# Splitting the left-over tokens one block ahead of their matmuls, into tiles of their own

## The chip, the core and the metric

The kernel runs on one core of one Trainium2 chip. The metric is device time in microseconds (us) for one whole execution. A core has a matrix engine (TensorE; PE in the profile, and PEld for its weight loads), a vector engine (VectorE, DVE), an activation engine (ScalarE, ACT), and a queue that issues DMA transfers (SP). Each engine works through its own instructions in order and waits for the others through semaphores.

## The reference, cut to what matters

A two-step attention makes one row of 512 numbers for each of 8 x 576 = 4608 tokens, and a feed-forward block with the Mish activation follows:

```python
p_packed = sm_attn(p, k, v)            # 32 packed rows per batch and head
out = sm_attn(q, p_packed, p_packed)   # batch 8, heads 8, seq 576, head_dim 64
x = out.transpose(0, 2, 1, 3).reshape(4608, 512)
h = x @ w_in                           # 512 -> 2048
g = h * np.tanh(softplus(h))           # Mish
return g @ w_out                       # 2048 -> 512
```

## The kernel before, in words

**Arithmetic.** A float32 operand of the large products is split into a high part (cast to a shorter float) and a low part (operand minus high part). Three matmuls, high x high, high x low, low x high, stand for one (`down_one`, L403 to L407). Every split therefore needs a copy that casts and a subtraction.

**Tiling.** The main loop (L501) runs over 8 batches x 16 pieces of 128 hidden features, called groups, and two further turns that drain it. One turn of the loop is called a block here, and f is the group's number within its batch. In block t the kernel

- computes the hidden values of group t in two halves of 288 tokens (`up`, L379): six matmuls each into a `ps_h` bank of PSUM, of which there are two, then Mish on ACT (L391);
- splits 512 of the 576 tokens into `g_hi` and `g_lo` on DVE (`halves`, L397, with L400 and L401);
- multiplies group t-2 (`dn` in the code; LAG is 2) with `w_out`, four chunks of 128 tokens, three matmuls each, into four PSUM accumulators held over all 16 groups of a batch (`down`, L419);
- moves the attention of the next batch a few steps on (`next(gen)`); these steps use the two-bank PSUM pool `ps_a`, ACT and DVE. In the blocks with f % 4 == 2, `packed_w` (L331) makes the next piece of the folded input weights, in the same pool.

**The left-over tokens.** 576 is not a multiple of 128: 64 tokens remain per batch. Mish for them goes to a tile `g_rest` (L393), four groups side by side. Two batches, an even and an odd one, are put together so that 64 + 64 fill 128 rows. When `dn` is the last of four groups of an odd batch (L542), `down_rest` (L437) splits both `g_rest` tiles (`split`, L357: two casts on ACT, L362, and two subtractions on DVE, L363), runs twelve matmuls into a `ps_a` bank, and copies the bank to, or adds it on, the tile `o_rest` (L446, L449). That happens 16 times: four odd batches with four sets of four groups. The block in which it happens has f = 5, 9, 13 of the same odd batch, or f = 1 of the batch after it. In the last batch, there being no next one, the fourth happens in the second draining turn.

**Buffers.** `split_tiles` (L354) hands out `g_hi` and `g_lo` tiles with GB = 3 buffers of each. `halves` and `split` take from the same three. At the time of a `down_rest`, groups t, t-1 and t-2 hold one each; group t-2 gives its own back with its last matmul, the one just ahead of `down_rest`.

**What sets the order.** Only PE's order is written out by hand (`manual_schedule`, L474): it follows the text of the loop. The order of ACT and DVE, and which of them makes an `nc.any` copy, is chosen when the kernel is built, by a planner that prefers what stands earlier in the text among the instructions that it takes to be ready. On the chip each engine then keeps its order. The lines at the end of a block read:

```python
            if grp:
                grp.up(1)
                grp.halves()
            if dn:
                down(dn, 3)
            ...
            if dn and dn.b % 2 == 1 and dn.f % 4 == 3:
                down_rest(dn)
```

Of the kernel before, what the change touches and what calls it, by code (L numbers as in the profile page):

```python
# [9 lines left out]
F32R = mybir.dt.float32r  # L10
# [7 lines left out]
GB = 3  # L18
# [10 lines left out]
def body(  # L29
# [16 lines left out]
    P = 128  # L46
# [8 lines left out]
    MAIN = NCH * P  # L55
# [8 lines left out]
    moe = ctx.enter_context(tc.tile_pool(name="moe", bufs=2))  # L64
# [38 lines left out]
    def psum(pool, shape, name):  # L103
        return pool.tile(shape, F32, name=name, tag="acc" if pool is ps_acc else "ps_a")
# [221 lines left out]
    def fetch_wi(b, c):  # L326
        for g in range(2):
            wis[b, c, g] = wts.tile([P, 2, FC], F32, name="wi", tag="w32", bufs=4)
            nc.sync.dma_start(out=wis[b, c, g], in_=w_in_f32[c][:, g])

    def packed_w(b, c):  # L331

        ppTb = batches[b].ppT
        ps = [ps_a.tile([P, FC], F32, name=f"ps_w{g}", tag="ps_a") for g in range(2)]
        for h in range(4):
            for g in range(2):
                row = ((h % 2) ^ g) * D
                nc.tensor.matmul(  # L338
                    out=ps[g][h * NP:(h + 1) * NP, :],
                    lhsT=ppTb[row:row + D, g, h * NP:(h + 1) * NP],  # L340
                    rhs=wis[b, c, g][row:row + D, h // 2, :],
                    start=True, stop=True,
                    tile_position=(row, h * NP),
                )
        halves = []
        for g in range(2):
            hi = wts.tile([P, FC], F32R, name="wp_hi", bufs=4)
            lo = wts.tile([P, FC], F32R, name="wp_lo", bufs=4)
            nc.scalar.copy(out=hi, in_=ps[g])  # L349
            nc.vector.tensor_tensor(out=lo, in0=ps[g], in1=hi.bitcast(F32), op=ALU.subtract)  # L350
            halves.append((hi, lo))
        return halves

    def split_tiles():  # L354
        return [moe.tile([P, MAIN], F32R, name=n, bufs=GB) for n in ("g_hi", "g_lo")]

    def split(*srcs):  # L357

        hi, lo = split_tiles()
        for n, src in enumerate(srcs):  # L360
            h, l = (x.rearrange("p (f u t) -> p u f t", u=len(srcs), f=src.shape[1])[:, n] for x in (hi, lo))
            nc.scalar.copy(out=h, in_=src)  # L362
            nc.vector.tensor_tensor(out=l, in0=src, in1=h.bitcast(F32), op=ALU.subtract)  # L363
        return hi, lo

    class Group:
# [30 lines left out]
        def halves(self):  # L397
            self.g = split_tiles()
            hi, lo = self.g
            nc.vector.tensor_copy(out=hi, in_=self.act)  # L400
            nc.vector.tensor_tensor(out=lo, in0=self.act, in1=hi.bitcast(F32), op=ALU.subtract)  # L401

    def down_one(acc, hi, lo, cs, f, start, stop):  # L403
        wh, wl = wo_hi[f], wo_lo[f]
        nc.tensor.matmul(out=acc, lhsT=hi[:, cs], rhs=wh, start=start, stop=False)  # L405
        nc.tensor.matmul(out=acc, lhsT=hi[:, cs], rhs=wl, start=False, stop=False)  # L406
        nc.tensor.matmul(out=acc, lhsT=lo[:, cs], rhs=wh, start=False, stop=stop)  # L407
# [11 lines left out]
    def down(grp, c):  # L419
        b, f, g = grp.b, grp.f, grp.g  # L420
        if f == 0 and c == 0:
            accs[:] = [ps_acc.tile([P, DO], F32, name=f"acc{i}", tag="acc") for i in range(NCH)]
        down_one(accs[c], g[0], g[1], slice(c * P, (c + 1) * P), f, f == 0, f == NF - 1)
        if f < NF - 1:
            return
        o = evac(accs[c], c)
        a = c * P
        while a < (c + 1) * P:
            n = a // R
            e = min((n + 1) * R, (c + 1) * P)  # L430
            si = 2 * (n % NI) + n // NI
            nc.sync.dma_start(out=out_v[b, si, a - n * R:e - n * R, :], in_=o[a - c * P:e - c * P, :])
            a = e

    rest = {}

    def down_rest(grp):  # L437

        i = grp.f // 4
        hi, lo = split(grp.g_rest[0][i], grp.g_rest[1][i])  # L440
        ps = psum(ps_a, [P, DO], "ps_rest")
        for t in range(4):
            down_one(ps, hi, lo, slice(t * P, (t + 1) * P), 4 * i + t, t == 0, t == 3)
        if i == 0:
            rest["o"] = moe.tile([P, DO], F32, name="o_rest", bufs=1)
            nc.scalar.copy(out=rest["o"], in_=ps)  # L446
            return
        o = rest["o"]
        nc.vector.tensor_tensor(out=o, in0=ps, in1=o, op=ALU.add)  # L449
        if i == NF // 4 - 1:  # L450
            for u in range(2):
                nc.sync.dma_start(
                    out=out_v[grp.b - 1 + u, SI - 1, R - REST:R, :], in_=o[u * REST:(u + 1) * REST, :]
                )

    def together(*gens):
        gens = list(gens)
        while gens:
            gens = [x for x in gens if next(x, "end") != "end"]
# [9 lines left out]
    def convert(n):  # L469
        for fn, *args in weights[:n]:  # L470
            fn(*args)
        del weights[:n]

    with tc.manual_schedule(engines={mybir.EngineType.PE}):  # L474
        for _ in range(8):
            nc.tensor.matmul(out=ps_warm, lhsT=still, rhs=still, start=True, stop=True)
        first = batches[0]
        first.load()
        convert(2)
        first.start(ps_a)  # L480
        together(first.score(0, ps_acc))
        first.exps(slice(0, 1))
        together(first.score(1, ps_acc))
        first.exps(slice(1, 2))
        together(first.turn(0, ps_a))
        convert(2)
        together(first.turn_weights(0, ps_acc))
        together(first.turn(1, ps_a))
        together(first.turn_weights(1, ps_acc))
        together(first.values(0, ps_acc), first.values(1, ps_acc))  # L490
        together(first.turn_values(0, ps_a), first.turn_values(1, ps_a))
        together(first.match(0, ps_acc), first.match(1, ps_acc))
        for g in range(2):
            first.weigh(slice(g, g + 1))
        wps = {(0, 0): packed_w(0, 0)}
        convert(5)
        batches[1].load()
        groups = []
        gen = iter(())
        g_rest = None  # L500
        for t in range(n_groups + LAG):  # L501
            b, f = divmod(t, NF)
            grp = None
            if t < n_groups:
                if f == 0:
                    if b % 2 == 0:
                        g_rest = ([], [])
                if f == (0 if b else 2) and b + 1 < B:
                    gen = batches[b + 1].attention()
                if f == 10 and b + 2 < B:  # L510
                    batches[b + 2].load()
                grp = Group(b, f, wps[b, f // 4], g_rest)
                grp.tiles()
            groups.append(grp)
            dn = groups[t - LAG] if t >= LAG else None
            if b == 0:
                convert(2)
            if dn:
                down(dn, 0)
            if grp:  # L520
                grp.up(0)
            next(gen, None)
            if dn:
                down(dn, 1)
                down(dn, 2)
            next(gen, None)
            if grp:
                grp.up(1)
                grp.halves()
            if dn:  # L530
                down(dn, 3)
            if grp and f % 4 == 2:
                nb, nch = divmod(b * (NF // 4) + f // 4 + 1, NF // 4)
                if nb < B:
                    if nb > b:
                        together(gen)
                    wps[nb, nch] = packed_w(nb, nch)
                    if nb + (nch + 1) // 4 and nb + (nch + 1) // 4 < B:
                        fetch_wi(nb + (nch + 1) // 4, (nch + 1) % 4)
            else:  # L540
                next(gen, None)
            if dn and dn.b % 2 == 1 and dn.f % 4 == 3:  # L542
                down_rest(dn)
# [26 lines left out]
```

## Time and profile before

| what | value |
|---|---|
| time of 3 runs | median 862.61 us, 859.67 to 862.83 |
| the profiled execution | 864.72 us, of which its span (first to last instruction) is 862.6 us |
| mean granted TensorE clock | 0.957 of full speed |
| PE busy | 91% of the span |
| DVE, ACT busy | 49%, 39% |
| DMA queue of the data | 34.2% of 16 DMA engines' span |

Durations below come from the profiled execution. In a row of the timeline the first number is the start in us from the span's start, the second how long it took; then follow the engine, the line of the kernel, the operation, what is written <- what is read, the shape, how many instructions of that kind are merged in the row, and in brackets how long the engine stood idle before and which instruction ended that. Matmuls overlap each other in the records, so that the distance from one start to the next is shorter than the duration. In a row of the stage table come the stretch, its length, the busy time of PE, PEld, DVE, ACT and POOL, each with its number of instructions, the granted clock of PE, the share of the DMA engines, and GB/s.

### The profile page before, as it was taken

To read this page: it belongs to the slowest core of one execution; us is meant where nothing else is said; L and a number is where in the kernel's file an instruction comes from. 1 tells how busy PE (TensorE), PEld (TensorE's weight loads), DVE (VectorE), ACT (ScalarE), POOL (GpSimd) and SP (SyncE) were. 2 spreads that over 40 slices of the span, in tenths; PEclk is the share of its full clock that TensorE was granted. 3 is DMA by queue.
4 is the path that set the end of the run, shared out by engine and by line. 5 is a ranking of instruction groups with operands and counts; after the bars stand their busy time and mean duration, and the time that the engine had idled before them with its cause. 6 is when DMAs were issued, how large, how long until landed. Compare 5 with 4: busy or idle time off the path is not lost.

```text
span 862.6 us, 13789 instructions
## 1 busy us (share of the span) xinstructions
PE 782.9 (91%) x5584; PEld 614.0 (71%) x5584; DVE 421.3 (49%) x812; ACT 335.2 (39%) x766; POOL 0.7 (0%) x6
## 2 busy tenths in 40 slices
PE   6508679999989999999989999999989999999997
PEld 4306567777767787777767777877767777887776
DVE  4788984743453335544453344544363344532332
ACT  3556673435332353335232353335242352332221
POOL 0000000000000000000000000000000000000000
PEclk9857879999989999999999999999999999999999
DMA  9957753243311433153311343144300431131002
GB/s 260 273 204 226 239 184 85 65 154 93 105 50 49 123 105 105 49 154 109 105 50 49 96 132 105 49 132 131 105 28 31 125 95 51 50 98 49 1 1 61
DMA packets 43966, 90.02 MB, mean 104 GB/s; under 512 B 8576, under 2 KB 27008, under 8 KB 43904
## 3 DMA queue, kind: packets, MB, share of 16 engines
q1 hardware_dynamic: 43904, 89.15, 34.2%
q8 instruction: 44, 0.72, 0.3%
q14 instruction: 18, 0.15, 0.1%
HBM read 75.50 MB, written 13.63 MB: 103 GB/s over the span
## 4 chain that ended last, share of the span: by engine, by line
PE 79%; DVE 7%; DMA 7%; ACT 4%; issue 2%; SPq 0%; DVEq 0%; ACTq 0%
PE ps_h L388 22%; PE acc L405 14%; PE acc L407 13%; PE acc L406 13%; PE ps_w L338 3%; PE ps_kq L118 3%; DMA w_st<-in_moe_w_in_dram 3%; PE ps_rest L407 2%; PE ps_s L127 2%; DMA w_st<-in_moe_w_out_dram 2%; PE ps_rest L406 2%; PE ps_rest L405 2%; PE ps_pp L209 1%; DVE g_lo L363 1%; DVE g_hi L400 1%
## 5 line engine op out<-in xcount | busy, mean ns | idle before, releaser
L391 ACT ACTIVATE g<-ps_h 128x288 f32<-128x288 f32 (+1 forms) x256 | 98.5, 385 | 322.6 <-PE ps_h L388 260.7
L405 PE MATMUL acc<-wo_hi,g_hi 128*128 128x512 f32 x512 | 217.5, 425 | 0.0
L406 PE MATMUL acc<-wo_lo,g_hi 128*128 128x512 f32 x512 | 204.0, 398 | 0.0
L407 PE MATMUL acc<-wo_hi,g_lo 128*128 128x512 f32 x512 | 203.7, 398 | 0.0
L400 DVE CAST g_hi<-g 128x512 fp32r<-128x512 f32 x128 | 54.6, 426 | 268.2 <-ACT g L391 268.2
L388 PE MATMUL ps_h<-aT_hi,wp_hi 128*128 128x288 f32 x512 | 159.2, 311 | 23.2 <-ACT aT_hi L263 22.6
L388 PE MATMUL ps_h<-aT_lo,wp_hi 128*128 128x288 f32 x512 | 152.9, 299 | 1.9 <-DVE aT_lo L264 1.9
L388 PE MATMUL ps_h<-aT_hi,wp_lo 128*128 128x288 f32 x512 | 152.9, 299 | 0.0
L405 PEld LDWEIGHTS acc<-wo_hi,g_hi 128*128 128x128 f32 x512 | 97.7, 191 | 42.9 <-issue 23.7
L388 PEld LDWEIGHTS ps_h<-aT_hi,wp_hi 128*128 128x128 f32 x512 | 97.9, 191 | 40.6 <-ACT aT_hi L263 24.1
L407 PEld LDWEIGHTS acc<-wo_hi,g_lo 128*128 128x128 f32 x512 | 97.4, 190 | 23.8
L388 PEld LDWEIGHTS ps_h<-aT_lo,wp_hi 128*128 128x128 f32 x512 | 98.2, 192 | 11.3 <-DVE aT_lo L264 2.6
L406 PEld LDWEIGHTS acc<-wo_lo,g_hi 128*128 128x128 f32 x512 | 98.1, 192 | 8.8
L388 PEld LDWEIGHTS ps_h<-aT_hi,wp_lo 128*128 128x128 f32 x512 | 98.1, 192 | 0.0
L401 DVE TENSOR_TENSOR g_lo<-g,g_hi 128x512 fp32r<-128x512 f32 x128 | 88.3, 690 | 6.1
L350 DVE TENSOR_TENSOR wp_lo<-ps_w,wp_hi 128x512 fp32r<-128x512 f32 x64 | 41.4, 684 | 21.2 <-ACT wp_hi L349 21.2
L349 ACT CAST wp_hi<-ps_w 128x512 fp32r<-128x512 f32 x64 | 34.4, 591 | 33.8 <-PE ps_w L338 33.8
L405 PE MATMUL ps_rest<-wo_hi,g_hi 128*128 128x512 f32 x64 | 29.4, 459 | 12.7 <-ACT g_hi L362 12.6
L407 PE MATMUL ps_rest<-wo_hi,g_lo 128*128 128x512 f32 x64 | 29.8, 466 | 8.7 <-DVE g_lo L363 8.7
L338 PE MATMUL ps_w<-wi,ppT 64*32 64x512 f32 x512 | 35.7, 606 | 0.0
L118 PE MATMUL ps_kq<-ident,k_t 96*128 96x96 f32 x192 | 26.6, 270 | 9.2 <-issue 5.5
L118 PE MATMUL ps_kq<-ident,q_t 96*128 96x96 f32 x192 | 27.0, 270 | 8.4 <-issue 3.1
(81 smaller groups left out, 725.4 us busy)
## 6 DMA issues: line engine op xcount, KB each, us to landing
wi<-w_in_f SPq DMA_DIRECT2D x56, 512.0 KB, 4.5
k_t<-in_k_dram SPq DMA_DIRECT2D x32, 288.0 KB, 3.7
q_t<-in_q_dram SPq DMA_DIRECT2D x32, 288.0 KB, 5.0
v_t<-in_v_dram SPq DMA_DIRECT2D x32, 288.0 KB, 3.5
w_st<-in_moe_w_in_dram SPq DMA_DIRECT2D x16, 512.0 KB, 5.3
w_st<-in_moe_w_out_dram SPq DMA_DIRECT2D x16, 512.0 KB, 4.4
out_dram<-o SPq DMA_DIRECT2D x24, 192.0 KB, 2.6
w_in_f<-wi SPq DMA_DIRECT2D x8, 512.0 KB, 5.0
```

Of the source, the lines that this page charges most:

```text
L118: nc.tensor.transpose(out=ps[:, h, :], in_=of_slot(src, g, h)[:, i, :], identity=ident[:R, :R])
L127: nc.tensor.matmul(out=ps[u][h * NP:(h + 1) * NP, :], lhsT=packT[u * D:(u + 1) * D, h * NP:(h + 1) * NP], rhs=xT[u * D:(u + 1) * D, :, h, ...
L338: nc.tensor.matmul(out=ps[g][h * NP:(h + 1) * NP, :], lhsT=ppTb[row:row + D, g, h * NP:(h + 1) * NP], rhs=wis[b, c, g][row:row + D, h // 2 ...
L349: nc.scalar.copy(out=hi, in_=ps[g])
L350: nc.vector.tensor_tensor(out=lo, in0=ps[g], in1=hi.bitcast(F32), op=ALU.subtract)
L388: nc.tensor.matmul(out=ps, lhsT=w[:, fs], rhs=a[:, g, cs], start=(n == 0), stop=(n == 5))
L391: nc.scalar.activation(out=self.act[:, hf * HALF:hf * HALF + m], in_=ps[:, :m], func=AF.Mish)
L400: nc.vector.tensor_copy(out=hi, in_=self.act)
L401: nc.vector.tensor_tensor(out=lo, in0=self.act, in1=hi.bitcast(F32), op=ALU.subtract)
L405: nc.tensor.matmul(out=acc, lhsT=hi[:, cs], rhs=wh, start=start, stop=False)
L406: nc.tensor.matmul(out=acc, lhsT=hi[:, cs], rhs=wl, start=False, stop=False)
L407: nc.tensor.matmul(out=acc, lhsT=lo[:, cs], rhs=wh, start=False, stop=stop)
```

## The change

The tile maker gets a name and a number of buffers. `halves` keeps its three buffers of `g_hi` and `g_lo`; `split` gets one buffer each of two new tiles, `r_hi` and `r_lo`. The call of `split` moves out of `down_rest`, where `dn.f % 4 == 3`, to the block before, where `dn.f % 4 == 2`: after the `halves` of that block's group and ahead of its `down(dn, 3)`. `down_rest` picks up the finished tiles.

```diff
-    def split_tiles():
-        return [moe.tile([P, MAIN], F32R, name=n, bufs=GB) for n in ("g_hi", "g_lo")]
+    def split_tiles(name="g", bufs=GB):
+        return [moe.tile([P, MAIN], F32R, name=f"{name}_{n}", bufs=bufs) for n in ("hi", "lo")]
 
     def split(*srcs):
 
-        hi, lo = split_tiles()
+        hi, lo = split_tiles("r", 1)
...
     def down_rest(grp):
 
         i = grp.f // 4
-        hi, lo = split(grp.g_rest[0][i], grp.g_rest[1][i])
+        hi, lo = rest["g"]
...
                 grp.up(1)
                 grp.halves()
+            if dn and dn.b % 2 == 1 and dn.f % 4 == 2:
+                rest["g"] = split(dn.g_rest[0][dn.f // 4], dn.g_rest[1][dn.f // 4])
             if dn:
                 down(dn, 3)
```

## The prediction

> **What bounds the kernel now.** I read the page first, for the span; then the groups of PE's instructions for the stretch from 200 us to the last matmul; then PE's waits; then the timeline around single places.
>
> ```profile
> span 862.6 us, 13789 instructions
> ```
>
> All left-over work lies behind 200 us. In that stretch PE's groups read as follows (line, engine, names, shape, count | busy us, mean ns | idle us ahead of them and who ended it):
>
> ```profile
> L405 PE MATMUL acc<-wo_hi,g_hi 128*128 128x512 f32 x439 | 183.6, 418 | 0.0
> ...
> L388 PE MATMUL ps_h<-aT_lo,wp_hi 128*128 128x288 f32 x430 | 126.6, 294 | 0.0
> L407 PE MATMUL ps_rest<-wo_hi,g_lo 128*128 128x512 f32 x64 | 29.8, 466 | 8.7 <-DVE g_lo L363 8.7
> L405 PE MATMUL ps_rest<-wo_hi,g_hi 128*128 128x512 f32 x64 | 29.4, 459 | 12.7 <-ACT g_hi L362 12.6
> ```
>
> The reader is to see that PE, the engine that sets the end, has no idle time to speak of in its large groups, and that the two that do wait are matmuls of `ps_rest`, the left-over tokens: first for the cast of L362, then for the subtraction of L363. These two lines are what the change moves. The view of PE's waits gives their number (us in total, times, longest):
>
> ```profile
> PE ps_h L388 <- ACT aT_hi L263: 22.6, 2, 17.0
> PE ps_rest L405 <- ACT g_hi L362: 12.6, 12, 2.8
> PE ps_rest L407 <- DVE g_lo L363: 8.7, 15, 1.3
> ```
>
> The wait above them, for the first batch's attention, lies at the start of the kernel and isn't touched. 15 of the 16 places wait: three each at f = 5, f = 9 and f = 1, and six with no attention beside them, at f = 13 and in the last batch. The sixteenth, in the draining turns, doesn't. Its split on ACT and then its first matmuls on PE show what a place costs when the split is done early:
>
> ```profile
> 849.49 0.71 ACT L362 CAST g_hi<-g_rest 128x256 fp32r<-128x256 f32 x2
> ```
> ```profile
> 854.89 0.39 PE L407 MATMUL acc<-wo_hi,g_lo 128*128 128x512 f32 x1
> 855.13 0.39 PE L405 MATMUL ps_rest<-wo_hi,g_hi 128*128 128x512 f32 x1
> 855.36 0.39 PE L406 MATMUL ps_rest<-wo_lo,g_hi 128*128 128x512 f32 x1
> ```
>
> There the matmuls start every 0.23 us, from the main product into the left-overs without a break. An ordinary place, in a block with no attention beside it, looks like this, PE first, then ACT, then DVE:
>
> ```profile
> 264.11 0.40 PE L407 MATMUL acc<-wo_hi,g_lo 128*128 128x512 f32 x1
> 265.07 0.50 PE L405 MATMUL ps_rest<-wo_hi,g_hi 128*128 128x512 f32 x1 [0.56 <-ACT g_hi L362]
> 265.40 0.40 PE L406 MATMUL ps_rest<-wo_lo,g_hi 128*128 128x512 f32 x1
> 266.18 0.50 PE L407 MATMUL ps_rest<-wo_hi,g_lo 128*128 128x512 f32 x1 [0.38 <-DVE g_lo L363]
> ```
> ```profile
> 264.31 0.71 ACT L362 CAST g_hi<-g_rest 128x256 fp32r<-128x256 f32 x2
> ```
> ```profile
> 265.37 0.75 DVE L363 TENSOR_TENSOR g_lo<-g_rest,g_hi 128x256 fp32r<-128x256 f32 x2
> ```
>
> The cast begins 0.20 us after the start of the last matmul that reads group t-2's buffer: it was waiting for that buffer, since the three are taken. PE then has the cast and the subtraction in front of it. The worst places, three of them, are those in the block with f = 9:
>
> ```profile
> 236.38 0.40 PE L407 MATMUL acc<-wo_hi,g_lo 128*128 128x512 f32 x1
> 239.60 0.80 PE L405 MATMUL ps_rest<-wo_hi,g_hi 128*128 128x512 f32 x1 [2.83 <-ACT g_hi L362]
> ```
> ```profile
> 236.00 1.17 ACT L252 ACTIVATE a<-a 128x1152 f32<-128x1152 f32 x1 [0.33 <-DVE a L249]
> 237.19 1.28 ACT L391 ACT_TABLE_LOAD   x1
> ...
> 238.84 0.71 ACT L362 CAST g_hi<-g_rest 128x256 fp32r<-128x256 f32 x2
> ```
>
> Here the buffer is free at about 236.6 us, but ACT is in the exponentials of the next batch's second softmax, then loads the table for Mish, and comes to the cast 2.2 us later. In the block with f = 1 it is DVE that is late:
>
> ```profile
> 290.57 0.40 PE L406 MATMUL ps_rest<-wo_lo,g_hi 128*128 128x512 f32 x1
> 292.28 0.50 PE L407 MATMUL ps_rest<-wo_hi,g_lo 128*128 128x512 f32 x1 [1.31 <-DVE g_lo L363]
> ```
>
> **What the waits cost now.** The idle time understates it, in three ways.
>
> Idle time: 12.6 + 8.7 = 21.3 us.
>
> Overlap: an undisturbed matmul takes 0.39 us by the record and the next starts after 0.23. A wait also loses the 0.16 that would have overlapped. 12 + 15 = 27 waits x 0.16 = 4.3 us.
>
> Refilling: after a wait the second matmul follows 0.33 us after the first (265.07 to 265.40) and not 0.23. 27 waits x 0.10 = 2.7 us. As a check, the ordinary place has 0.56 + 0.38 + 2 x 0.16 + 2 x 0.10 = 1.46 us, and by starts alone, from 264.11 to 266.18, it has 2.07 - 3 x 0.23 = 1.38, to which the refill behind 266.18 (0.10) comes: 1.48.
>
> The clock: the stage table for the stretches around four of the places shows the granted clock of PE (the number ahead of the last two):
>
> ```profile
> 238.93:245.76 6.83, 6.00 (x13) 4.30 (x14) 5.68 (x11) 1.71 (x5) 0.00 (x0) 0.50 0.00 0
> 485.00:488.10 3.10, 1.74 (x9) 1.01 (x9) 2.65 (x7) 1.10 (x3) 0.00 (x0) 1.00 0.78 246
> 488.10:491.50 3.40, 3.40 (x10) 2.66 (x9) 0.00 (x0) 0.00 (x0) 0.00 (x0) 0.50 0.04 11
> 434.00:436.90 2.90, 0.73 (x2) 0.30 (x2) 2.58 (x7) 1.68 (x5) 0.00 (x0) 1.00 0.00 0
> 436.91:440.32 3.41, 3.20 (x8) 2.53 (x9) 2.64 (x4) 0.67 (x1) 0.00 (x0) 0.50 0.00 0
> 631.50:634.88 3.38, 1.52 (x5) 0.97 (x6) 3.06 (x8) 1.15 (x5) 0.00 (x0) 1.00 0.00 0
> 634.88:638.29 3.41, 3.41 (x9) 2.64 (x8) 1.36 (x3) 0.67 (x1) 0.00 (x0) 0.50 0.00 0
> 236.80:239.60 2.80, 0.00 (x0) 0.00 (x0) 2.08 (x4) 2.72 (x6) 0.00 (x0) 0.88 0.00 0
> 265.00:268.60 3.60, 3.15 (x12) 2.29 (x13) 1.12 (x3) 0.02 (x1) 0.00 (x0) 1.00 0.00 0
> ```
>
> After the three 2.83 us waits at f = 9, and after one of the three at f = 1, PE works at half clock for 3.4 or 6.8 us. After an ordinary place (last row) it doesn't. PE was busy 6.00 + 3.40 + 3.20 + 3.41 = 16.0 us at half clock; work that takes 16.0 us there takes 8.0 at full clock, so at most 8 us are lost. A part of that busy time is fixed latency, which need not halve, so I take 7.
>
> Together 21.3 + 4.3 + 2.7 + 7 = 35.3 us, all on PE. At f = 9 alone it is 3 x (2.83 + 0.16 + 0.10) = 9.3 for the first wait, about 2 for the second (of the 8.7, six ordinary places take 6 x 0.38 and three at f = 1 take 3 x 1.31, which leaves 2.5 for those at f = 5 and f = 9, and overlap and refill come to it), and 12.6 x 0.5 = 6.3 less a little for the clock: 17 us.
>
> The Trainium skill, page "TensorE: Matmul & The Clock Gate", section "HAM oscillation — how this bites in real kernels", has the clock fall only when PE stands idle for longer than about 3.4 us. This trace differs: 2.83 us idle had half clock behind it three times, and 1.31 us (487.7 us, the third row) once. By that rule the half clock isn't the doing of these waits, and the saving would be without its 7 us; it is a rival below.
>
> **The change, part by part.**
>
> Removed: the wait for group t-2's buffer. With tiles of its own the split needs only `g_rest`, finished a block earlier: the fourth of the groups, dn + 1, had its Mish in the block before the one in which the split now stands. The single `r` buffer was last read four blocks earlier, so it adds no wait. Saved at the 12 places outside f = 9: all that they cost now, 35.3 - 17 = 18.
>
> Moved: per place two casts on ACT, 0.71 us together, and two subtractions on DVE, 0.75, to the block before; no DMA goes with them. That block has f = 4, 8, 12 or 0, without exponentials. The matmuls come at the end of the next block, which first has twelve main matmuls (12 x 0.23 = 2.8 us) and two halves of the up product to do. So casts and subtractions, 1.5 us one behind the other, have twice their time or more. The stretches in which I expect them (one of each kind):
>
> ```profile
> 203.50:205.60 2.10, 2.10 (x17) 1.90 (x16) 1.07 (x2) 0.51 (x2) 0.00 (x0) 1.00 0.03 7
> 231.40:233.90 2.50, 2.50 (x27) 1.82 (x27) 2.43 (x5) 0.00 (x0) 0.00 (x0) 1.00 0.00 0
> 260.10:262.60 2.50, 2.50 (x15) 2.14 (x14) 0.86 (x2) 0.41 (x1) 0.00 (x0) 1.00 0.00 0
> 283.50:286.00 2.50, 2.50 (x19) 2.27 (x18) 1.07 (x2) 1.44 (x5) 0.00 (x0) 1.00 0.00 0
> ```
>
> ACT has 1.06 to 2.50 us free in each, enough for 0.71. DVE has over 1.0 us free in three, enough for 0.75; only behind f = 8 (second row, 2.43 of 2.50 busy) does it push something back: the transposes and the maximum of the second softmax, by up to 0.75 us. Queued behind it are the exponentials and the Mish of f = 9. The Mish is needed for a `ps_h` bank only two halves later, and DVE is rid of the same 0.75 us one block on. If that cover is gone, each of the three costs 0.75.
>
> Bounds of the moved part: nothing at the lower end (it can't gain, being the same instructions), and at the upper end 16 x (0.71 + 0.75) = 23 us if PE waited for all of it. Nearest is the last place, whose split ran at 849.49 us, 5 us ahead of its matmuls, with no wait of PE's behind it: nothing. I take 0.5 us at each of the three f = 8 places: 1.5.
>
> What is late next at f = 9: PE's twelve matmuls now begin at once and the following block comes 6 us sooner, towards `packed_w` at f = 10. That wants two `ps_a` banks, one of which is free only when the add of L449 has run on DVE, which is then in the softmax. I expect it to fit between two steps of that chain.
>
> Sum: 35.3 - 1.5 = 34 us (33.8). The profiled execution's 864.72 us would become 831; it lies 2.1 over the median of the runs, 862.61, so that the median would become 829.
>
> **The rivals.**
>
> *The waits at f = 9 stay in another form.* The add of L449, or the Mish of f = 10, sits in its engine's order behind the softmax's chain, and PE waits for a PSUM bank. For it: that chain holds ACT with the exponentials of 236.00 us, and DVE has its subtractions, sums and transposes of it (DVE is busy for 5.68 of 6.83 us in the first row of the stage table). Against: the planner chooses the order anew. Saving 34 - 17 = 17: 846 us.
>
> *The clock falls without these waits.* If the half-clock stretches come from something else near by, 7 us remain: 836 us. Against it is that each follows a wait directly.
>
> *The change doesn't do what it says.* The planner leaves the casts where they were in ACT's order, since nothing asks for them sooner: 863 us. Against: they stand ahead in the text and are ready.
>
> *Slower.* The subtraction waits on DVE for casts that stand on ACT behind exponentials and table loads; DVE keeps its order, so the split of the next group, the copies of the attention and the `wp_lo` behind it wait too, and PE after them. One such place costs what f = 9 costs now, 17 / 3 = 5.7 us. Of the 16 new places 9 have attention beside them (f = 4, 8 and 0, three each). From 35.3 / 5.7 = 6.2, that is with 7 of the 9, the kernel is slower; with 8 it is 862.6 - 35.3 + 8 x 5.7 = 873 us. Against: ACT's exponentials lie in other blocks, as the busy time of ACT in the last four rows shows.
>
> **How the numbers follow.** Forecast 0.76, waits in another form at f = 9 0.07, clock 0.06, no effect 0.05, slower 0.06. About 0.5%, or 4.3 us, is what a measurement of this kernel can tell from no change: faster 0.89, same 0.05, slower 0.06. The range: at the low end the fastest run before, 859.67, less 35.3, which is 824; at the high end 842, past the clock rival and a third of the way from it to the whole of the upper bound of the moved part (829 + 23 = 852); no effect, slower and most of the f = 9 rival lie outside.
>
> **What would show it.** In the changed profile the `ps_rest` groups should have under 2 us of idle time instead of 21.3, their mean duration should fall from about 460 ns to about 400, the casts of L362 should stand about one block ahead of the first `ps_rest` matmul, and the granted clock should hold 1.0 from 200 us on. I am wrong if PE's idle time shows up at `ps_w` or `ps_h` behind f = 9, if half-clock stretches remain, or if the main product's groups wait for `g_lo`.

## The result, and the profile after

The changed kernel takes 823.0 us (median; 821.91 to 824.24, 4 runs) against 861.24 us (859.67 to 862.83, 4 runs): the ratio is 0.9556, with a 95% interval of 0.9529 to 0.9584. The forecast was 829, with a range from 824 to 842; the time lies 1 us below the range. The saving is 38 us where 34 were forecast; with one more run the median before is 1.4 us lower than in the table ahead of the prediction.

The profiled execution took 822.64 us, its span 820.9. PE's groups, from 200 us to the last matmul (columns as in the prediction):

```profile
L405 PE MATMUL acc<-wo_hi,g_hi 128*128 128x512 f32 x435 | 181.5, 417 | 0.0
...
L405 PE MATMUL ps_rest<-wo_hi,r_hi 128*128 128x512 f32 x64 | 25.7, 402 | 0.0
L407 PE MATMUL ps_rest<-wo_hi,r_lo 128*128 128x512 f32 x64 | 25.2, 394 | 0.0
```

The idle time of 12.7 and 8.7 us ahead of these groups is gone, and a `ps_rest` matmul takes 394 to 402 ns on average, no longer 459 and 466. The view of PE's waits has no entry between 200 and 820 us. The place that was worst, in a block with f = 9, on PE's timeline:

```profile
229.55 0.39 PE L407 MATMUL acc<-wo_hi,g_lo 128*128 128x512 f32 x1
229.78 0.39 PE L405 MATMUL ps_rest<-wo_hi,r_hi 128*128 128x512 f32 x1
230.02 0.39 PE L406 MATMUL ps_rest<-wo_lo,r_hi 128*128 128x512 f32 x1
```

The main product runs into the left-overs with its 0.23 us from start to start. The stage table gives the granted clock (third from the end) for the same two stretches of either kernel, first the changed one, then the one before:

```profile
200.00:818.00 618.00, 616.26 (x4456) 492.67 (x4454) 276.25 (x510) 228.34 (x551) 0.00 (x0) 1.00 0.28 84
84.00:131.00 47.00, 38.15 (x230) 30.88 (x229) 42.24 (x88) 33.62 (x67) 0.00 (x0) 0.83 0.66 207
```
```profile
200.00:857.90 657.90, 636.33 (x4494) 501.33 (x4492) 278.62 (x517) 230.86 (x560) 0.00 (x0) 0.99 0.26 79
84.00:131.00 47.00, 35.25 (x198) 27.55 (x197) 40.47 (x85) 30.17 (x60) 0.00 (x0) 0.80 0.64 202
```

No half clock is left between 200 and 818 us. The second row of each pair tells something else: between 84 and 131 us, long before the first left-over matmul, the changed kernel has put 230 matmul records behind it where the kernel before had 198. What moved there shows in ACT's timeline of the changed kernel:

```profile
86.77 0.20 ACT L393 ACTIVATE g_rest<-ps_h 128x64 f32<-128x64 f32 x1
87.00 0.41 ACT L362 CAST r_hi<-g_rest 128x256 fp32r<-128x256 f32 x1
```
```profile
194.40 0.43 ACT L362 CAST r_hi<-g_rest 128x256 fp32r<-128x256 f32 x1
...
206.42 0.41 ACT L362 CAST r_hi<-g_rest 128x256 fp32r<-128x256 f32 x1 [2.09 <-PE ps_rest L406]
```

The text puts the two casts of the first place side by side, one block ahead of matmuls that begin at 203.57 us. The planner took the even batch's half as soon as its data were there, in batch 0, 117 us ahead, while the weights are still being converted; only the odd batch's half (194.40 us) stands near them, 9 us ahead. The last row is the even half of the second place, which is used at 229.78 us: it too is cast early, as soon as the first place's last matmul on `r_hi` frees that tile.

To tell the two apart I cut the span at one matmul, the first of the up product in block 8 of batch 0 (block 0 marks the start of the main loop). The marks, with the start of the last matmul, in the kernel before and in the changed one:

```profile
55.27 0.61 PE L388 MATMUL ps_h<-aT_hi,wp_hi 128*128 128x288 f32 x1 [17.03 <-ACT aT_hi L263]
...
132.11 0.29 PE L388 MATMUL ps_h<-aT_hi,wp_hi 128*128 128x288 f32 x1
...
857.70 0.40 PE L407 MATMUL ps_rest<-wo_hi,g_lo 128*128 128x512 f32 x1
```
```profile
53.49 0.61 PE L388 MATMUL ps_h<-aT_hi,wp_hi 128*128 128x288 f32 x1 [15.50 <-ACT aT_hi L263]
...
126.43 0.29 PE L388 MATMUL ps_h<-aT_hi,wp_hi 128*128 128x288 f32 x1
...
816.02 0.40 PE L407 MATMUL ps_rest<-wo_hi,r_lo 128*128 128x512 f32 x1
```

From block 8 to the last matmul it was 725.6 us and is 689.6: 36.0 less. This is the late part, and all of the 16 places lie in it. Cut further, at the matmul ahead of each place, it falls apart into 17.18 us for the three places at f = 9, 8.77 for the six with no attention beside them (1.46 or 1.47 each), 6.60 for the three at f = 1 and 3.45 for the three at f = 5. From block 0 to block 8 it was 76.8 and is 72.9: 3.9 less. The 1.8 us ahead of block 0 is no effect of the change: the order of every engine is the same there, and the mark moves from 52.2 to 55.3 us between the executions below.

### The profile page after: what moved, and what is told of

It reads as the page before. It is cut to its first block, busy times and chain, and to the rows that moved or that the text cites. A ratio compares the mean times of both kernels' runs of the same rounds, so it can differ in the third digit from the quotient of the medians.

```text
span 820.9 us, 13745 instructions
## 1 busy us (share of the span) xinstructions
PE 768.2 (94%) x5584; PEld 610.4 (74%) x5584; DVE 420.6 (51%) x812; ACT 336.0 (41%) x766; POOL 0.7 (0%) x6
## 4 chain that ended last, share of the span: by engine, by line
PE 88%; DMA 5%; DVE 4%; issue 1%; ACT 1%; SPq 0%; ACTq 0%
PE ps_h L388 25%; PE acc L405 16%; PE acc L407 14%; PE acc L406 14%; PE ps_kq L118 4%; DMA w_st<-in_moe_w_in_dram 4%; PE ps_w L338 4%; PE ps_s L127 3%; PE ps_rest L405 2%; PE ps_rest L407 2%; PE ps_rest L406 2%; PE ps_pp L209 1%; PE ps_a L200 1%; DMA k_t<-in_k_dram 1%; DMA w_st<-in_moe_w_out_dram 1%
## 5 line engine op out<-in xcount | busy, mean ns | idle before, releaser
L118 PEld LDWEIGHTS ps_kq<-ident,k_t 96*128 96x128 f32 x192 | 23.1, 158 | 16.4 <-issue 6.4
L118 PEld LDWEIGHTS ps_kq<-ident,q_t 96*128 96x128 f32 x192 | 22.6, 154 | 13.1 <-issue 4.6
```

The costliest lines, as they stand in the source:

```text
L118: nc.tensor.transpose(out=ps[:, h, :], in_=of_slot(src, g, h)[:, i, :], identity=ident[:R, :R])
```

## The experiments

My theory after the result had two parts. One: the late 36 us are the waits at the old place with their half clock, as predicted, and nothing came back. Two: the rest is an early gain, made by the planner's new order of ACT and DVE in batch 0, which follows from the early cast (the early-order theory). The rivals: chance for the early part; the buffer, or the place in the text, as the cause of the late part. "Early" is block 0 to block 8 of batch 0, "late" is from there to the start of the last matmul, both from the one profiled execution of each kernel. Each ratio is to runs of the kernel before beside that kernel, whose median was 861.24 to 861.66 us.

| run | tiles | call of `split` | early us | late us | time us | ratio, 95% interval |
|---|---|---|---|---|---|---|
| before | g, 3 | old place | 76.8 | 725.6 | 861.2 | |
| changed | own | a block ahead | 72.9 | 689.6 | 823.0 | 0.9529 to 0.9584 |
| e1 changed, again | own | a block ahead | 71.8 | 689.6 | 822.75 | 0.9530 to 0.9575 |
| e2 | own | a block ahead, tied there | 75.4 | 689.6 | 826.71 | 0.9576 to 0.9621 |
| e3 | own | old place | 72.5 | 689.6 | 822.68 | 0.9530 to 0.9574 |
| e4 | g, 4 | old place | 75.2 | 725.6 | 861.88 | 0.9995 to 1.0021 |
| e5 | g, 3 | a block ahead | 76.4 | 689.6 | 826.35 | 0.9564 to 0.9599 |
| e6 | g, 4 | a block ahead | 76.2 | 689.6 | 825.6 | 0.9556 to 0.9591 |
| e7 | own | old place, tied there | 76.7 | 716.4 | 853.73 | 0.9875 to 0.9926 |
| e8 | g at f = 9, else own | old at f = 9, else ahead | 72.1 | 708.3 | 840.68 | 0.9732 to 0.9769 |
| e9 | own at 1st place, else g | ahead at 1st, else old | 71.5 | 725.2 | 856.95 | 0.9927 to 0.9967 |
| e10 | g at 1st place, else own | old at 1st, else ahead | 75.0 | 690.7 | 826.31 | 0.9569 to 0.9621 |
| e11 changed, conversion late | own | a block ahead | 72.4 | 689.6 | 821.54 | 0.9509 to 0.9553 |

**e1: the changed kernel again.** No edit.

> The changed kernel once more, as a measure for the others. Prediction's theory (the waits at the old place, 35.3 us gross): at most 36 us below the kernel before, about 825 us against 861; what it measured beyond that, 38 to 42, would be chance. Rival (the planner, which now casts the even batch's half as early as 87 us, has put the conversion of the weights into a better order): 38 us or more again, about 823, and the first up matmul of block 8 of batch 0 at 126 to 127 us again, where the kernel before had 132.1.

822.75 us, and block 8 at 124.9 us, earlier than the 126 to 127 expected. The early gain is there again.

**e2: own tiles, the casts tied to their place in the text.** `issue_after` keeps the casts on ACT behind the block's last Mish.

```diff
-                nc.scalar.activation(
+                rest["mish"] = nc.scalar.activation(
                     out=self.g_rest[...][...], in_=ps[:, m:], func=AF.Mish
                 )
...
-                rest["g"] = split(...)
+                with tc.issue_after(rest["mish"].ins) if grp else ExitStack():
+                    rest["g"] = split(...)
```

> Own tiles, split one block ahead as in the change, but the casts are tied on ACT behind the last Mish of that block, so that they can't be cast earlier than the text has them. The order of all engines up to 190 us is that of the kernel before. Prediction's theory: the same as the changed kernel, 823 to 825 us. Rival (early order): the 36 us of the waits alone, so 2 to 4 us slower than the changed kernel, 825 to 827, with block 8 of batch 0 at about 132 us.

826.71 us, and its interval of the ratio begins where that of e1 ends. The late part is the changed kernel's to 0.1 us; the early part is 75.4. ACT and DVE keep the order of the kernel before until the first of these casts, at 198.94 us. The rival that I had named for it, the early order, holds.

**e3: own tiles, split called at the old place.**

```diff
-            if dn and dn.b % 2 == 1 and dn.f % 4 == 2:
-                rest["g"] = split(...)
...
-        hi, lo = rest["g"]
+        hi, lo = split(grp.g_rest[0][i], grp.g_rest[1][i])
```

> Tiles of their own, but split is called where the kernel before calls it, just ahead of its matmuls. If the place in the text matters (prediction: one block ahead): the casts stay behind exponentials and Mish, the three f = 9 places and the three f = 1 places keep most of their waits, about 845 to 855 us. Rival (the tag decides: with tiles of their own the planner may cast as soon as the tile and the data are there): the same as the changed kernel, 823 us, and no idle time at ps_rest.

The same as the changed kernel, 822.68 us, with the even half cast at 88.08 us:

```profile
88.08 0.41 ACT L362 CAST r_hi<-g_rest 128x256 fp32r<-128x256 f32 x1
```

With tiles of their own, the move in the text adds nothing to the time: the planner has already made it.

**e4: four g buffers, all else as before.** `GB = 4` for `GB = 3`.

> The kernel before with four g buffers for three: the split no longer has to wait for group t-2's buffer, and the planned order of every engine is the same as before, instruction by instruction. Prediction's reading (at the ordinary places the cast was waiting for that buffer): the cast can begin about 0.2 to 0.5 us earlier at 9 places, some 3 us less, 858. Rival (ACT comes to the cast only behind its last Mish, which ends at the same moment): no change, 861, idle time at ps_rest 21 us as before.

No change: 861.88 us, ratio 1.0008. The order of every engine is the same as before, instruction by instruction, so that only the wait for the buffer is taken away. The ordinary place on ACT, PE and DVE:

```profile
260.56 0.22 ACT L393 ACTIVATE g_rest<-ps_h 128x64 f32<-128x64 f32 x1
260.66 0.71 ACT L362 CAST g_hi<-g_rest 128x256 fp32r<-128x256 f32 x2
```
```profile
260.57 0.40 PE L407 MATMUL acc<-wo_hi,g_lo 128*128 128x512 f32 x1
261.42 0.50 PE L405 MATMUL ps_rest<-wo_hi,g_hi 128*128 128x512 f32 x1 [0.46 <-ACT g_hi L362]
```
```profile
261.22 0.69 DVE L401 TENSOR_TENSOR g_lo<-g,g_hi 128x512 fp32r<-128x512 f32 x1
261.83 0.75 DVE L363 TENSOR_TENSOR g_lo<-g_rest,g_hi 128x256 fp32r<-128x256 f32 x2
```

The cast now starts 0.09 us after the last main matmul, not 0.20, and PE's first wait is 0.46 us, not 0.56. But the subtraction stands behind `g_lo` of the group on DVE and comes no earlier, so the second wait takes back what the first gave: in total the first waits fall from 12.6 to 11.2 us, and the second ones rise from 8.7 to 10.0. With this order of ACT and DVE the buffer was no cost; the place in the order was.

**e5 and e6: the call a block ahead, in shared g tiles, three and four of them.**

```diff
-        hi, lo = split_tiles("r", 1)
+        hi, lo = split_tiles()
```

e6 has `GB = 4` besides.

> The call one block ahead, but the tiles still from the three shared g buffers. The split then takes the buffer of the group whose down product ends that block, and the next group's split has to wait for the end of its block. Theory 1 (place is what counts): the ps_rest waits are gone all the same, since a block is long enough for a cast that starts at its end; about 825 us. Theory 2 (the buffer counts): the casts come at the end of the block ahead, and the next halves late; new waits at g_lo of the main product or at ps_h, 16 of about 1 us, 840 us.

> The call one block ahead, four shared g buffers and no tiles of their own; casts stand one block ahead in ACT's order and the early order is that of the kernel before. Theory 1 (place): as the pinned kernel, 825 us. Theory 2 (own tag needed): ps_rest waits remain, above 840 us.

826.35 and 825.6 us. Both late parts are those of the changed kernel, and PE has no wait between 200 and 820 us in either; not even the three shared buffers bring one. Theory 1 of either expectation, the place, holds for the late part. So there either half of the change is enough alone: the call a block ahead in the shared tiles (e5), or own tiles with the call at the old place (e3). Neither e5 nor e6 casts in batch 0, and their early parts are long.

**e7: own tiles at the old place, the casts tied on ACT behind their block's last Mish.** The edit of e2, on e3.

> Own tiles, called at the old place, and the casts tied on ACT behind the last Mish of their own block, so that the buffer's wait is gone but the casts stand where they stood. Theory (the place in ACT's order is the whole cost): as the kernel before, within 3 us, 858 to 862. Rival (the buffer was a cost of its own): 850 or less.

853.73 us: between the two expectations, late part 9.2 us shorter. PE's first waits, those for ACT, are as in e4, but DVE, which wasn't tied, has moved one of the two subtractions ahead of `g_lo`:

```profile
261.24 0.42 DVE L363 TENSOR_TENSOR r_lo<-g_rest,r_hi 128x256 fp32r<-128x256 f32 x1
261.58 0.68 DVE L401 TENSOR_TENSOR g_lo<-g,g_hi 128x512 fp32r<-128x512 f32 x1
262.19 0.42 DVE L363 TENSOR_TENSOR r_lo<-g_rest,r_hi 128x256 fp32r<-128x256 f32 x1
```

The waits of PE in e7:

```profile
PE ps_rest L405 <- ACT r_hi L362: 11.2, 9, 2.8
PE ps_rest L407 <- DVE r_lo L363: 5.6, 12, 0.8
```

The second waits fall to 5.6 us, and the half clock behind the waits from 17.1 us in the kernel before to 6.8. So this run doesn't isolate the buffer, which e4 does.

**e8: the f = 9 places the old way.** With `shared=True`, `split` takes its tiles from the shared g buffers.

```diff
-            if dn and dn.b % 2 == 1 and dn.f % 4 == 2:
+            if dn and dn.b % 2 == 1 and dn.f % 4 == 2 and dn.f != 6:
...
-        hi, lo = rest["g"]
+        hi, lo = split(..., shared=True) if i == 1 else rest["g"]
```

> The changed kernel, but the second of the four sets (f = 9) is split as before, at its old place in shared g tiles: 3 of the 16 places. By the prediction's sum they cost 17 us, 11 in waits and 6 in half clock behind the 2.83 us waits: 840 us, with half clock for 3.4 us or more behind each. If the clock has nothing to do with the waits (the rule of no fall under 3.4 us idle): 834 us, with the granted clock at 1.0 there.

840.68 us, late part 18.7 us longer. The set holds four places, not three: the fourth, in the last batch, is an ordinary one of 1.5 us, which leaves 17.2 for the three, where the prediction had 17. The half clock is back with the waits; here the stretches behind them in the stage table:

```profile
231.50:238.30 6.80, 6.17 (x14) 4.39 (x15) 4.11 (x9) 1.09 (x3) 0.00 (x0) 0.50 0.00 0
426.00:429.40 3.40, 3.40 (x9) 2.68 (x9) 2.11 (x4) 0.67 (x1) 0.00 (x0) 0.50 0.00 0
617.20:620.60 3.40, 3.40 (x9) 2.62 (x9) 2.59 (x4) 0.67 (x1) 0.00 (x0) 0.50 0.00 0
```

The rival by which the clock has nothing to do with these waits falls.

**e9 and e10: the first place alone the new way, and all but the first.** The test `(dn.b, dn.f) == (1, 2)` is put beside, or against, `dn.f % 4 == 2`, and the other places split in shared g tiles at the old place, as in e8.

> The kernel before, with the first of the 16 places alone done the new way (own tiles, called a block ahead); its even half is cast at about 87 us. Early-order theory: block 8 of batch 0 begins about 72.3 us after block 0 and not 76.1, and with the 1.1 us of that place the time is 5 us below the kernel before, 856 to 857. Rival (the early gain is chance or comes from elsewhere): 1.1 us, 860 to 861.

> The changed kernel, with the first of the 16 places alone done the old way. Its even half isn't cast in batch 0; that of the second place may be, later in batch 0 (about 125 us). Early-order theory: the early part as in the kernel before (76 us from block 0 to block 8), 823 + 3.8 + 1.1 = 827 to 828 us. Rival: 824.

e9's marks, to be held against those of the kernel before:

```profile
52.71 0.61 PE L388 MATMUL ps_h<-aT_hi,wp_hi 128*128 128x288 f32 x1 [15.38 <-ACT aT_hi L263]
...
124.17 0.29 PE L388 MATMUL ps_h<-aT_hi,wp_hi 128*128 128x288 f32 x1
```

One early cast of 0.41 us, moved by the change at one place of 16, shortens the early part to 71.5 us and the time by 4.7 us (861.65 in the runs of the kernel before beside it). The late part gets 0.4 us shorter, not 1.1: half clock fell on two f = 1 places in that execution and on one in the kernel before, 1.5 us more, and lasted 3.4 us at the first f = 9 place and not 6.8, 0.8 us less. Without the first place (e10) the late gain is there less 1.1 us, and the early gain isn't: 75.0 us. Its first early cast, that of the second place, comes at 126.15 us, 1 us ahead of block 8. The early-order theory holds in both directions. Over all runs, the six with that cast (changed, e1, e3, e8, e9, e11) have early parts of 71.5 to 72.9 us, the seven without of 75.0 to 76.8; the means are 3.8 us apart.

**e11: the conversion of the weights called at the end of the block.**

```diff
-            if b == 0:
-                convert(2)
             if dn:
                 down(dn, 0)
...
                 down_rest(dn)
+            if b == 0:
+                convert(2)
```

> The changed kernel, with the conversion of the weights called at the end of each block of batch 0 and not at its head, so that the casts of the folded weights and the attention's copies stand ahead of it in the text. If the early waits come from conversions standing ahead of those on ACT and DVE: some 2 to 6 us less than the changed kernel, 817 to 821. If they come from the weights' transfers: the same, 823, or more, since the conversions and their transfers begin later.

821.54 us, below the changed kernel, but the intervals overlap and its early part, 72.4 us, lies between the 71.8 and 72.9 of that kernel's two profiles. Inconclusive; at best 1.5 us. It is no version that clearly beats the changed kernel.

What in the new order brings the early 3.8 us shows in part. At block 7 of batch 0, PE's next attention matmul waits for the subtraction that makes `wp_lo`, the low half of the folded weights; that subtraction reads `ps_w`, which by the kernel's text holds both banks of `ps_a`, and the matmul writes into one of them. Before, after, and in e9:

```profile
125.85 0.55 PE L118 MATMUL ps_kq<-ident,q_t 96*128 96x96 f32 x4 [2.27 <-DVE wp_lo L350]
```
```profile
121.72 0.47 PE L118 MATMUL ps_kq<-ident,q_t 96*128 96x96 f32 x3 [1.05 <-DVE wp_lo L350]
```
```profile
119.45 0.55 PE L118 MATMUL ps_kq<-ident,q_t 96*128 96x96 f32 x4 [2.09 <-DVE wp_lo L350]
```

ACT and DVE before, then ACT and DVE after, at the casts and subtractions that this waits for:

```profile
121.52 0.66 ACT L312 CAST wo_hi<-wo 128x512 fp32r<-128x512 f32 x1
122.03 0.74 ACT L296 ACTIVATE wround<-w_st 128x512 int32<-128x512 uint32 x1
122.62 1.12 ACT L349 CAST wp_hi<-ps_w 128x512 fp32r<-128x512 f32 x2
```
```profile
123.90 1.29 DVE L299 SCALAR_TENSOR_TENSOR wo<-w_st,wo 128x512 int32<-128x512 int32 x2
125.11 1.28 DVE L350 TENSOR_TENSOR wp_lo<-ps_w,wp_hi 128x512 fp32r<-128x512 f32 x2
```
```profile
119.08 1.07 ACT L349 CAST wp_hi<-ps_w 128x512 fp32r<-128x512 f32 x2 [0.61 <-PE ps_w L338]
120.04 0.64 ACT L312 CAST wo_hi<-wo 128x512 fp32r<-128x512 f32 x1
```
```profile
120.98 1.28 DVE L350 TENSOR_TENSOR wp_lo<-ps_w,wp_hi 128x512 fp32r<-128x512 f32 x2
```

Before, two steps of the weights' conversion stand on ACT ahead of the folded weights' casts; after, the casts go first. The wait is 2.27 to 2.31 us in all seven kernels without the early cast, and 1.05 or 1.06 in five of the six with it: 1.2 us of the 3.8. e9 is the exception. It waits 2.09 us, and its early part is the shortest all the same: the 10.3 us ahead of this wait (from 107.05 us) show no half clock, where every other kernel has 3.4 to 6.0 us of it in the same stretch. Counted from block 0, the matmul behind this wait starts after 66.7 to 68.2 us in the six and 70.2 to 71.7 in the seven, so that most of the gain is made by then. How it divides into waits, order and half clock differs from one execution to the next and stays open. Why one early cast makes the planner order the rest better was not tried either: it looks like luck of a plan and not a rule.

## Why the prediction was wrong, point by point

**The late waits: right.** Idle time, overlap, refill and clock were put at 35.3 us; every kernel that got rid of them without touching the early order (e2, e5, e6) or with it (e1, e3, e11) is 36.0 shorter in the late part. The idle time alone, 21.3, would have missed 15 us of it. The places bear the terms out: 17.2 us at f = 9 where the sum had 17, 18.8 at the others where it had 18, and 1.46 at an ordinary place, as worked out there.

**What comes back: too high.** I took 1.5 us for the three f = 8 places. Nothing came back in the late part: no wait of PE's stands between 200 and 820 us, and the rival of a new wait at `packed_w` didn't come up.

**The start of the kernel: wrong, and the step that put the time out of the range.** "Moved: per place two casts on ACT ... to the block before": I took the call's place in the text for the place of the casts, though the plan of ACT and DVE is free to go ahead of it, as I had written of the planner under the rivals. From it followed "it can't gain, being the same instructions": the moved part was held to be at least nothing and taken as 1.5 us lost, all ahead of the first place as unchanged, and the low end of the range as the fastest run before less 35.3. The cast at 87 us changed the order in batch 0, and e2, e9 and e10 show that the early gain comes and goes with it; over all profiles it is 3.8 us on average. Without it the change stays inside the range: e2, e5 and e6, with the late gain alone, take 825.6 to 826.7 us. Nothing in the prediction says whether such a cast would help or harm; that it helped was luck. 36.0 + 3.8 = 39.8 is what the profiles give without the chance at the start; the medians have 38.2, and each profile is a single execution.

**The buffer: wrong as a cause.** The prediction read the 0.20 us between the last main matmul and the cast as the wait for group t-2's buffer. e4 takes this wait away, the cast comes 0.11 us earlier, and nothing is gained: ACT comes from its Mish only then, and the subtraction stands behind `g_lo` on DVE. What the own tiles do is let the plan move: e4 has buffers enough and keeps the old order, while e3, at the same place in the text, casts in batch 0. That the planner hands out tiles of one name in the order of the text would explain it; this is argued from the orders and not shown.

**The clock: right.** e8 brings the half clock back with the waits. In e7, where the 2.83 us waits have next to no second wait behind them, two of the three were followed by it and one wasn't. The Trainium skill, page "TensorE: Matmul & The Clock Gate", section "HAM oscillation — how this bites in real kernels", sets the limit at an idle gap of about 3.4 us. In the kernel before, e4, e8 and e9 all twelve waits of 2.83 us had half clock with them, so here the measurement decides against the rule.

## What to carry to other kernels

Before costing a call that is moved in the text, ask which engines really follow the text; where a planner orders an engine, look for how far ahead the data would let it go, and expect other stages to change with it. A tile name of its own can be worth more than another buffer: at the same place in the text it gave 822.7 us (e3), a fourth shared buffer 861.9 (e4). And price a wait of PE by the starts of its matmuls, with what the clock does behind it: here 21.3 us of idle time were 36.0 us of time.

## What the runs showed of the hardware

A wait on PE of 2.83 us with a second one of 0.15 to 0.65 us about 1 us behind it had half clock for 3.4 or 6.8 us in twelve cases of twelve (the kernel before, e4, e8, e9); in three of them it had begun before the first wait was over (238.93 us in the kernel before, whose wait ended at 239.60). The 2.83 us alone had it in two cases of three (e7). A single wait of 1.30 to 1.41 us had it in four cases of nine (one of three in the kernel before and in e4, two of three in e9), each at an f = 1 place, and one of 0.80 us in none of three (e7). So the three f = 1 places of the kernel before, with the same wait, cost 1.7, 3.2 and 1.7 us. The half-clock stretches behind 200 us begin 197.98, 51.20 and 146.77 us apart there, which is 58, 15 and 43 times 3.413; why one wait brings it on and another doesn't stays open.
